# Attention and softplus FFN on one core: four buffers in place of two for the tile of reciprocals

## Chip, cores and metric

One core of a Trainium2 chip runs the whole program. The metric is the device time of one launch in microseconds (us); the median of several launches is compared. Engines are named as the profile names them: PE (TensorE matmul), PEld (TensorE weight load), DVE (VectorE), ACT (ScalarE), POOL (GpSimd), SP (SyncE, which issues nearly all DMAs).

## What is computed

Windowed attention over 8 batches, 8 heads, 576 tokens and head size 64, and behind it a feed-forward block with softplus on 4608 tokens. Float32 throughout.

```python
scores = scale * np.matmul(q, k.transpose(0, 1, 3, 2))        # heads 0-3: the last 32 keys;
scores = np.where(masks, scores, -1e9)                        # heads 4-7: every 4th of the last 128
attn = np.exp(scores - max) ; attn = attn / (attn.sum() + 1e-09)
x = (attn @ v) -> [4608, 512]
h = x @ w_in                                                  # 512 -> 2048
g = np.maximum(h, 0.0) + np.log1p(np.exp(-np.abs(h)))
out = g @ w_out                                               # 2048 -> 512
```

## The kernel before, in words

**Precision by parts.** A float32 operand of the feed-forward block is split into a high and a low part of the type fp32r, and a product takes three matmuls: high by high, high by low, low by high. Each of these matmuls has a stationary operand of 128x128 and a moving operand of 128 partitions by 512 columns (2048 bytes in a partition). In what follows "moving" is the operand that `matmul` gets as `rhs` (L228).

**Stages.** The 4608 tokens are nine chunks of 512. Chunks 0 to 2 are done plainly, in 48 slots (`RUNS`, L43: a chunk and one of 16 blocks of the hidden layer). A slot is twelve matmuls `h_ps<-xh/xl,parts` (`h_part`, L659), then ScalarE and VectorE make the softplus and its parts gh and gl (`activated` L672, `softplus` L679, `early_high` L1141, `g_low` L693), and two slots later (`LAG`) twelve matmuls `o_ps<-gh/gl,parts` (`o_matmuls`, L717). The first slots stand in an order written out by hand (`OPENING`, L93), which also decodes the weights; the rest is planned.

Chunks 3 to 8 are done as three supers of two chunks with a seven-product scheme for block matrices (`PRODUCTS`, L798). A super has 56 units of twelve matmuls (`unit`, L1258): 28 of the first half (moving operand: a block of x, `x<-a_h`, `y<-s_l` and so on) and 28 of the second half (moving operand g: `x<-g,ring`, `y<-g,ring`, `z<-g,ring`). Units are numbered on from super to super, so the second halves are units 28 to 55, 84 to 111 and 140 to 167. The weights of a unit come by DMA into one of five ring tiles. In a second half the two parts of the moving operand rotate over three pairs of tiles by u%3 (`moving_of`, L1248, with the tags of `MOVING`, L1227). Of the twelve matmuls of a unit, eight read the high part and four the low part (L1266).

```python
MOVING = (("w15_1", "n1"), ("n2", "n3"), ("n4", "n5"))      # L1227: high part, low part
for wp, xp in ((0, 0), (0, 1), (1, 0)):                      # L1266: xp is the part of the moving operand
```

Couples of attention groups of later chunks run in between as visits to TensorE (`s_ps`, `a_ps`), and jobs that prepare sums of weight blocks (`job`, L1068) run on GpSimd, VectorE and ScalarE and are stored by DMA (`w_t<-cast`).

**Order.** Everything behind the opening is a `Task` with a cost, options of engines and keys that it reads and writes; `planned` (L1459) puts them in order once, and each engine keeps that order. For the reciprocals the keys are ("ri", 0) and ("ri", 1) (L1026 and L1037): the divisor of a group is planned behind the normalisation that last read its key.

**The tile that the change touches.** `divisor` (L434) writes ri (128x8 float32, 32 bytes in a partition) with `reciprocal` (L442). It is read by `divide` (L444, in the opening, always with `nc.vector` there: the words `Pv` of `OPENING`) and by `normalized` (L548).

**Where tiles lie.** The pools are opened in the order `const`, `wk`, `dec`, `ep`, `gp` (L130 to L136) and lie one behind the other in each partition, each tag with as many places as it has buffers. At `switch` (L1231) `dec`, `ep` and `gp` are closed and `late` is opened where `dec` began. In bytes of a partition:

- `const`: begins at 1152 = 9 x 128, behind a DMA scratch of 1024 and four constants of 32. Its tags take 2816 (k2), 2560 (k), 2048 or 4096 bytes, all multiples of 128. Among them are xh and xl, the blocks of x, the ring tiles, all g_of tiles, the spare e on xl01 and w15_1.
- `wk`: nm, sm and ri, two buffers of 32 each, and mask, two buffers of 1024.
- `dec`: three buffers of 2048 for a. `ep`: two of 2048 for e of the slots. `gp`: pt, gh and gl (two each), g_x and g_y, 2048 or 2560 each.
- `late`: n0 (the other spare e), n1 to n5, 4096 each but n2 on its first use as d (2048). n1 to n4 serve the last six jobs first (b, d and cast), then n1 to n5 are g tiles.

Of the kernel before, what the change touches and what calls it, by code (L numbers as in the profile page):

```python
# [14 lines left out]
F32 = mybir.dt.float32  # L15
# [9 lines left out]
P = 128  # L25
# [8 lines left out]
NB = 2 * CH // P  # L34
# [81 lines left out]
def tile_windowed_attention_softplus_ffn(  # L116
# [15 lines left out]
    wk = ctx.enter_context(tc.tile_pool(name="wk", bufs=2))  # L132
# [23 lines left out]
    def pin(ins):  # L156

        tc.keep_in_program_order(ins)
        pinned[0] = ins
# [154 lines left out]
    class Group:  # L314
# [118 lines left out]

        def divisor(self):  # L434
            sm = self.sm
            self.ri = ri = wk.tile([P, NB], F32, name="ri")
            pin(nc.vector.tensor_scalar(
                out=sm, in0=sm, scalar1=1.0e-9, scalar2=1.0, op0=ALU.add, op1=ALU.mult
            ))
            if self.planned:  # L440
                sm, ri = sm.rearrange("p (r t h) -> p h t r", r=2, t=2), ri.rearrange("p (h t r) -> p h t r", h=2, t=2)
            pin(nc.vector.reciprocal(out=ri, in_=sm))  # L442
# [343 lines left out]
    for word in OPENING.split():  # L786
        name = word[:3] if word[0] == "D" and word[1] != "l" else word.rstrip("0123456789_")
# [856 lines left out]
```

## Time and profile before

| what | us |
|---|---|
| median of 3 runs | 829.82 |
| the runs | 828.8, 829.82, 832.06 |
| the profiled execution | 830.7 |
| its span, first to last instruction | 828.9 |
| TensorE matmul busy, of the span | 808.5 (98%) |
| VectorE busy | 663.9 (80%) |
| ScalarE busy | 500.8 (60%) |
| GpSimd busy | 188.3 (23%) |

The profile is one execution. Busy time of PE is the time in which at least one matmul was in the pipeline, and the duration of a single matmul (some 390 ns) overlaps with its neighbours'; how fast the matmuls follow one another is read from the chain of work that ended last, where consecutive matmuls of one output are merged to one piece with their count and the time that they took on the chain. Releasers of waits are inferred from semaphores. DMA share is the mean busy share of the core's 16 DMA engines.

### The profile page before, as it was taken

Reading aid. Unit: us, or ns where it says so; the run is one execution under the profiler, and the core shown is the slowest. Engines: PE = TensorE matmul, PEld = TensorE weight load, DVE = VectorE, ACT = ScalarE, POOL = GpSimd, SP = SyncE. Lnnn points to the kernel's source line nnn. Section 1 sums busy time; section 2 is a strip of 40 time slices with the busy share of each in tenths; the row PEclk is TensorE's granted clock in tenths of the full one; section 3 lists DMA queues with packets and bytes.
Section 4 is the critical chain, followed back from the end, with each engine's and each line's share of the span. In section 5 each row is a group of like instructions: output and inputs, shape, how many; then the busy total and the mean of one; then the engine's idle time right before and its main releaser. Section 6 shows DMA issues by size and latency. Waiting matters only on the chain.

```text
span 828.9 us, 19650 instructions
## 1 busy us (share of the span) xinstructions
PE 808.5 (98%) x7834; PEld 651.6 (79%) x7835; DVE 663.9 (80%) x967; ACT 500.8 (60%) x1122; POOL 188.3 (23%) x132
## 2 busy tenths in 40 slices
PE   6699999999999999999999999999999999999998
PEld 3577888888888888888777888888888888888886
DVE  5699899966687866898889887897997946768974
ACT  5587778745666644597786413888933516774410
POOL 0000000053043224655213202202024302222410
PEclk7899999999999999999999999999999999999999
DMA  9589994668879773999988999879988675655563
GB/s 330 192 290 357 368 314 132 231 209 267 276 236 290 229 214 135 361 348 368 336 292 285 327 335 323 300 234 345 304 271 291 226 243 190 202 186 196 183 214 136
DMA packets 118490, 218.94 MB, mean 264 GB/s; under 512 B 11520, under 2 KB 53632, under 8 KB 118400
## 3 DMA queue, kind: packets, MB, share of 16 engines
q1 hardware_dynamic: 117968, 216.97, 77.5%
q8 instruction: 62, 1.02, 0.5%
q10 hardware_dynamic: 432, 0.72, 0.3%
q14 instruction: 28, 0.23, 0.1%
HBM read 162.07 MB, written 55.57 MB: 263 GB/s over the span
## 4 chain that ended last, share of the span: by engine, by line
PE 89%; DMA 4%; DVE 3%; ACT 2%; issue 1%; SPq 0%; ACTq 0%; DVEq 0%
PE y L229 22%; PE o_ps L229 17%; PE h_ps L229 16%; PE z L229 14%; PE x L229 14%; PE s_ps L229 3%; PE a_ps L229 3%; DMA w_t<-cast 2%; DMA v<-vp 1%; DVE g_of L928 1%; DVE g L928 1%; DMA raw<-w 1%; DMA x_full<-rows 1%; ACT e L1296 1%; ACT s L425 1%
## 5 line engine op out<-in xcount | busy, mean ns | idle before, releaser
L928 POOL TENSOR_TENSOR g_of<-g_of 128x1024 f32<-128x1024 f32 x33 | 79.3, 2403 | 263.9 <-DVE g_of L1299 133.9
L928 DVE TENSOR_TENSOR g<-g_of,g 128x1024 fp32r<-128x1024 f32 x84 | 122.3, 1462 | 16.0 <-ACT g L960 15.2
L960 ACT CAST g<-g_of 128x1024 fp32r<-128x1024 f32 x61 | 63.7, 1047 | 111.2 <-PE z L229 42.6
L229 PE MATMUL o_ps<-gh,parts 128*128 128x512 f32 x384 | 130.8, 399 | 0.0
L229 PE MATMUL h_ps<-xh,parts 128*128 128x512 f32 x384 | 129.7, 396 | 0.0
L229 PE MATMUL y<-g,ring 128*128 128x512 f32 x432 | 102.5, 395 | 0.0
L1296 ACT ACTIVATE e<-e 128x1024 f32<-128x1024 f32 x96 | 101.1, 1057 | 1.7
L229 PEld LDWEIGHTS y<-g,ring 128*128 128x128 f32 x432 | 80.9, 188 | 19.0
L928 POOL TENSOR_TENSOR b<-parts 128x512 f32<-128x512 f32 x29 | 40.7, 1403 | 217.5 <-DVE parts L223 148.3
L229 PEld LDWEIGHTS o_ps<-gh,parts 128*128 128x128 f32 x384 | 71.9, 187 | 17.8
L229 PEld LDWEIGHTS h_ps<-xh,parts 128*128 128x128 f32 x384 | 72.7, 189 | 16.5 <-DVE e L681 0.4
L425 ACT ACTIVATE s<-s,nm 128x64 f32<-128x64 f32 x224 | 74.8, 336 | 6.7 <-DVE nm L416 6.7
L229 PE MATMUL o_ps<-gl,parts 128*128 128x512 f32 x192 | 75.8, 395 | 0.0
L229 PE MATMUL h_ps<-xl,parts 128*128 128x512 f32 x192 | 75.6, 394 | 0.0
L229 PE MATMUL x<-g,ring 128*128 128x512 f32 x288 | 68.2, 395 | 0.4 <-DVE g L928 0.4
L229 PE MATMUL z<-g,ring 128*128 128x512 f32 x288 | 68.1, 394 | 0.1
L229 PEld LDWEIGHTS x<-g,ring 128*128 128x128 f32 x288 | 53.9, 188 | 13.4 <-DVE g L928 0.8
L229 PE MATMUL z<-s_h,ring 128*128 128x512 f32 x192 | 63.2, 390 | 1.2 <-DMA ring<-w_b 1.2
L229 PEld LDWEIGHTS z<-g,ring 128*128 128x128 f32 x288 | 54.0, 188 | 13.1 <-DVE g L928 0.6
L928 DVE TENSOR_TENSOR g_of<-y,temp 128x512 f32<-128x512 f32 x60 | 39.9, 684 | 30.1 <-PE y L229 29.9
L229 PE MATMUL y<-s_h,ring 128*128 128x512 f32 x192 | 63.7, 392 | 0.0
L229 PE MATMUL x<-a_h,ring 128*128 128x512 f32 x192 | 63.3, 391 | 0.0
(111 smaller groups left out, 1517.7 us busy)
## 6 DMA issues: line engine op xcount, KB each, us to landing
ring<-w_t SPq DMA_DIRECT2D x96, 512.0 KB, 4.2
ring<-w_b SPq DMA_DIRECT2D x72, 512.0 KB, 4.7
raw<-w SPq DMA_DIRECT2D x64, 256.0 KB, 5.8
w_t<-cast SPq DMA_DIRECT2D x64, 256.0 KB, 5.1
w_b<-parts SPq DMA_DIRECT2D x48, 256.0 KB, 4.3
v<-vp SPq DMA_DIRECT2D x14, 512.0 KB, 5.3
x_full<-vp SPq DMA_DIRECT2D x14, 512.0 KB, 6.2
turned<-sq SPq DMA_DIRECT2D x112, 64.0 KB, 3.2
```

Of the source, the lines that this page charges most:

```text
L229: tc.keep_in_program_order(nc.tensor.matmul(**kw))
L425: pin(nc.scalar.activation(out=self.blocks[:, t], in_=src, func=AF.Exp, bias=self.nm[:, t : t + 1], scale=1.0 / 8.0 if self.masked else 1. ...
L928: pin((nc.gpsimd if name == "POOL" else nc.vector).tensor_tensor(out=dst, in0=a, in1=b, op=op))
L960: pin(nc.scalar.copy(out=dst, in_=src))
L1296: pin(nc.scalar.activation(out=to(), in_=of(), func=func, **kw))
```

## The change

The tile ri is given four buffers of its own in place of the pool's two. In a partition `wk` becomes 2 x 32 = 64 bytes longer, and all tiles of `mask`, `dec`, `ep`, `gp` and `late` move up by 64 bytes. Nothing else is changed.

```diff
         def divisor(self):
             sm = self.sm
-            self.ri = ri = wk.tile([P, NB], F32, name="ri")
+            self.ri = ri = wk.tile([P, NB], F32, name="ri", bufs=4)
```

## Rows read from the trace of the kernel before

**Rows 1.** The page: busy us (share) xinstructions by engine; the chain by engine.

```profile
PE 808.5 (98%) x7834; PEld 651.6 (79%) x7835; DVE 663.9 (80%) x967; ACT 500.8 (60%) x1122; POOL 188.3 (23%) x132
...
PE 89%; DMA 4%; DVE 3%; ACT 2%; issue 1%; SPq 0%; ACTq 0%; DVEq 0%
```

**Rows 2.** Waits of PE and PEld, 80 to 829 us: us, times, longest us.

```profile
PE z L229 <- DMA ring<-w_b: 1.2, 1, 1.2
...
PEld z L229 <- DVE temp L928: 1.6, 1, 1.6
PEld x L229 <- DVE g L928: 0.8, 1, 0.8
```

**Rows 3.** Busy us (instructions) PE, PEld, DVE, ACT, POOL; PE clock; DMA share; GB/s.

```profile
320.00:330.00 10.00, 10.00 (x45) 8.07 (x44) 8.23 (x10) 5.71 (x9) 7.16 (x5) 1.00 0.12 44
...
340.00:350.00 10.00, 10.00 (x106) 8.12 (x107) 9.05 (x14) 5.95 (x8) 4.70 (x5) 1.00 1.04 401
...
405.00:445.00 40.00, 38.29 (x404) 29.84 (x403) 35.24 (x46) 28.41 (x58) 9.61 (x4) 1.00 0.86 299
...
420.00:440.00 20.00, 19.87 (x85) 15.82 (x86) 19.97 (x25) 15.66 (x25) 2.41 (x1) 1.00 0.80 274
```

**Rows 4.** The chain, start us and us: matmuls on blocks of x.

```profile
333.12 2.74 PE x L229 x12
...
670.90 2.76 PE x L229 x12
673.66 2.72 PE z L229 x12
...
709.02 2.72 PE x L229 x12
```

**Rows 5.** The chain: early slots, both products.

```profile
165.70 2.80 PE o_ps L229 x12
168.50 2.74 PE h_ps L229 x12
...
200.55 2.80 PE o_ps L229 x12
```

**Rows 6.** The chain: the last second half, 28 units on g in seven rows.

```profile
747.10 11.14 PE x L229 x48
758.24 11.10 PE z L229 x48
769.34 11.15 PE y L229 x48
...
813.88 11.15 PE y L229 x48
```

**Rows 7.** The tile ri: ns min/median/max, first and last start us, forms.

```profile
L442 DVE RECIPROCAL ri<-sm x36: 202/204/206, 14.5 to 614.5; 128x8 f32<-128x8 f32 x36
L554 DVE TENSOR_TENSOR normal<-a_ps,ri x28: 637/681/693, 162.4 to 624.1; 128x512 f32<-128x512 f32 x28
L445 DVE TENSOR_TENSOR s<-s,ri x8: 681/684/693, 14.8 to 71.0; 128x512 f32<-128x512 f32 x8
```

**Rows 8.** The chain: first and last piece of 60 o_ps matmuls before 81 us.

```profile
48.44 2.80 PE o_ps L229 x12
...
78.07 2.30 PE o_ps L229 x9
```

**Rows 9.** Tiles e and g, ns min/median/max; the page's group: busy us, mean ns.

```profile
L1296 ACT ACTIVATE e<-e x96: 1039/1061/1067, 345.2 to 752.0; 128x1024 f32<-128x1024 f32 x96
...
L928 DVE TENSOR_TENSOR g<-g_of,g x84: 1170/1220/3458, 411.4 to 817.8; 128x1024 fp32r<-128x1024 f32 x84
...
L928 DVE TENSOR_TENSOR g<-g_of,g 128x1024 fp32r<-128x1024 f32 x84 | 122.3, 1462 | 16.0 <-ACT g L960 15.2
```

**Rows 10.** DMA issues: count, KB each, median us from issue to landing.

```profile
w_t<-cast SPq DMA_DIRECT2D x64, 256.0 KB, 5.1
w_b<-parts SPq DMA_DIRECT2D x48, 256.0 KB, 4.3
```

## The prediction, made before the changed kernel ran

> **What bounds the kernel now.** I read the busy times and the chain first, then TensorE's waits, then the busy times by stretch, and last the chain piece by piece. The first two say that TensorE is the bound: it is busy 98% of the span and holds 89% of the chain [rows 1]. From 80 us to the end the longest of its waits on other engines and DMAs are 1.2 us of matmuls and 1.6 us of weight loads [rows 2]. So a nanosecond taken off a big matmul after 80 us is a nanosecond off the end, unless an engine behind it cannot follow. In 405:445 one cannot: TensorE is busy 38.29 of 40 us there, and within it, in 420:440, VectorE is busy 19.97 of 20 [rows 3].
>
> The piece-by-piece chain is the view that decides this case. Every big matmul is 128x128 by 512 columns, and they come in twelves. The reader is to compare the time of twelve:
> - twelve on blocks of x (the first halves of the supers): 2.72 us [rows 4];
> - twelve of the output projection of the early slots (o_ps): 2.80 us, and the twelve h_ps after them 2.74 us [rows 5];
> - 48 in the second halves of the supers (moving operand g): 11.14, 11.10 or 11.15 us [rows 6], where four times 2.72 would be 10.88.
>
> [...] What differs is where the moving operand lies. The x blocks and xh, xl lie in `const`; gh and gl lie in `gp`; g lies in `late`, but for one of its six tiles, which is w15_1 in `const`. By the sizes of the tiles, `const` ends on a multiple of 128 bytes, `wk` takes 6 x 32 + 2 x 1024 = 2240 = 17 x 128 + 64 bytes, and so every tile of `dec`, `ep`, `gp` and `late` begins 64 bytes past a multiple of 128, and none of `const` does.
>
> The rows test this against the rival reading, that a freshly written operand is slow. Units of twelve rotate over three pairs of g tiles. With u%3 = 1 or 2 both tiles are in `late`; with u%3 = 0 the high part, read by 8 of 12 matmuls, is w15_1. If only the address counts, a full `late` unit costs 2.80 and a u%3 = 0 unit 2.72 + 0.08 x 4/12 = 2.747. The last second half starts at unit 140, so its seven groups of four hold one, two, one, one, two, one, one units of the cheap kind. That gives 3 x 2.80 + 2.747 = 11.147 or 2 x 2.80 + 2 x 2.747 = 11.094. The rows are 11.14, 11.10, 11.15 and, at the end, 11.15; the three left out there are 11.14, 11.10, 11.15 [rows 6]. Seven of seven fall as the address says, while w15_1 is written just before its use like the others. **So 64 bytes off cost 80 ns in twelve matmuls, 6.7 ns in each.**
>
> **The change part by part.**
> - *Four buffers of ri.* `wk` grows by 2 x 32 bytes to 2304 = 18 x 128. The readers of ri are the product at L445 and the normalisation at L554, both on VectorE, and so is its writer L442 [rows 7]: reuse of a buffer was already ordered by that engine, so no wait goes. The planner's keys are still ("ri", 0) and ("ri", 1), so its order stays. No instruction and no DMA is added or moved past a queue. 0 us; there is nothing to hide.
> - *Early slots.* RUNS has 48 slots, each with twelve h_ps and twelve o_ps. Sixty o_ps matmuls, five slots' worth, stand before 80 us [rows 8]; 43 slots come after. A pair costs 2.80 + 2.74 = 5.54 [rows 5] and should cost 2 x 2.72 = 5.44; the 0.02 on h_ps is the change-over from a shifted operand, seen as 2.76 too in the first twelve after a g phase [rows 4]. 43 x 0.10 = **4.3 us**. If the 0.02 belongs to h_ps itself, it is 43 x 0.08 = 3.4.
> - *Opening, five slots.* TensorE shares the chain with other engines there; between 0 and 5 x 0.10 = 0.5 I take the middle, **0.25 us**.
> - *Second halves of the supers.* The last one runs 813.88 + 11.15 - 747.10 = 77.93 us [rows 6] against 28 x 2.72 = 76.16: 1.77 us. Three of them: 5.3, and with the change-over of the x twelves behind them (2.76 and 2.74 against 2.72 [rows 4]) **5.4 us**.
> - *What VectorE takes back.* In 420:440 it is full [rows 3], so units 28 to 35 can't come sooner by their own saving: 8 x 1.77/28 = 0.5 us lost: **-0.5 us**; nothing lost if VectorE's waits shrink with TensorE's. What is late next there is the low part of g.
> - *VectorE, ScalarE, GpSimd.* e lies alternately at a shifted and at an unshifted address in the supers, yet all 96 activations take 1039 to 1067 ns [rows 9]. 0 us, with at most 28/1061 of a ScalarE that does not bind.
> - *The DMA-full stretch from 340 us* (share 1.04 [rows 3]) could swallow the 4.3 us won before it. But the DMAs are at share 0.12 in 320:330, and fill only when TensorE leaves the early slots. I count no loss; the rival below prices it.
> - *DMAs that touch the moved pools.* Of the 64 transfers w_t<-cast, 24 read a `late` tile. The nearest rows, 256 KB each, are 5.1 us to landing for these and 4.3 us for w_b<-parts, which reads `const` alone [rows 10]. So the bounds are 24 x 0.8 = 19 us of landing time either way, and it lies beside TensorE as long as a block is stored before the ring loads it back. I take 0, because the two rows differ in stage and share as much as in address. If that cover were gone, it would show in the stretch of rival 1.
>
> Sum: 4.3 + 0.25 + 5.4 - 0.5 = 9.45 us, against the profiled execution of 830.7 us (span 828.9 and 1.8 around it). That execution is 0.1% above the median of the runs, 829.82, so I take the sum from the median: **820.4 us**.
>
> [...] The trace shows 2.72 against 2.80 for the same twelve at two addresses. [...]
>
> **The rivals.**
> 1. *The win before 333 us is lost at 405:445.* If DMAs and VectorE there keep their time of day, TensorE waits for ring and g, and only the later savings count: 5.4 - 0.5 = 4.9, so **824.9 us**. For it: TensorE idles there already [rows 2, 3]. Against: the DMAs are nearly empty just before [rows 3].
> 2. *The change does nothing to the matmuls.* The address is not the cause, but something else that `gp` and `late` share, such as lying last in the partition: **829.8 us**. Against it stands w15_1; for it, that one tile is the only witness inside one phase.
> 3. *Slower: VectorE and GpSimd meet more often.* The place is the subtraction that makes the low part of g: 1220 ns at the median, 3458 at worst [rows 9], when GpSimd's sums run beside it. A meeting that nothing covers costs 2.24 us. More than 9.45/2.24, so five, uncovered new ones turn the sign; eight give 17.9 - 9.45 = 8.5 us more, **838 us**. Against it: the 84 instructions already lose (mean 1462, [rows 9]) 84 x 0.24 = 20 us, and TensorE's waits on VectorE come to a few microseconds at most [rows 2].
>
> **How the numbers follow.** About 0.5% is what a measurement of this kernel can tell from no change: 4.1 us, so faster means below 825.7. Forecast 0.82; rival 1 0.10; rival 2 0.05; rival 3 0.03. Nearly all of the first and about 0.06 of rival 1 are faster: 0.88. Rival 2 and the rest of rival 1 are the same: 0.09; slower 0.03. The low end is the sum with no loss to VectorE and the opening whole (4.3 + 0.5 + 5.4 = 10.2, 819.6) less a little for the runs' scatter: 818.8. The high end takes in rival 1 at its own figure: 825.
>
> **What would show it.** Right: o_ps and h_ps in twelves of 2.72, 48 on g in 10.88, VectorE's and ScalarE's durations as before, the last second half 1.8 us shorter, and TensorE's wait near 405:445 about 0.5 us longer. Wrong: twelves on g still at 2.80 (rival 2); a new TensorE wait of some 4 us in 405:445 (rival 1); low parts of g above 1462 ns in the mean with TensorE waiting for them (rival 3).

## The result, and the profile after

The changed kernel takes 820.52 us at the median (818.43 to 822.06), beside 829.17 us for the kernel before on the same chips: a ratio of 0.9891 with a 95% interval of 0.9871 to 0.9911. The forecast was 820.4 us. One execution further down, of the kernel with everything on a multiple of 256, took 1322.09 us at a mean granted clock of 0.556; its ratio goes by the three others, and no chain of it is shown, because the trace is of that one.

The profiled execution of the changed kernel spans 818.7 us. Its page first, busy time by engine and the chain by engine, to be read against [rows 1]:

```profile
span 818.7 us, 19651 instructions
PE 799.4 (98%) x7835; PEld 651.8 (80%) x7835; DVE 660.3 (81%) x967; ACT 501.0 (61%) x1122; POOL 189.9 (23%) x132
...
PE 89%; DMA 5%; DVE 3%; ACT 1%; issue 1%; POOL 0%; SPq 0%; POOLq 0%; DVEq 0%; ACTq 0%
```

TensorE is as much the bound as before, with 9.1 us less of busy time. The instructions are the same and stand in the same order on every engine. (The one matmul more is a record that the trace before lacks.)

The chain piece by piece, start us and us, shows where the time went. The early slots, against [rows 5], the first halves, against [rows 4], and the last second half, against [rows 6]:

```profile
165.93 2.72 PE h_ps L229 x12
168.65 2.72 PE o_ps L229 x12
...
179.53 1.41 PE a_ps L229 x91
180.94 2.97 PE o_ps L229 x12
183.91 2.72 PE h_ps L229 x12
...
328.51 2.72 PE x L229 x12
...
662.50 2.72 PE x L229 x12
...
738.66 10.88 PE x L229 x48
749.54 10.88 PE z L229 x48
...
803.94 10.89 PE y L229 x48
```

Every twelve that neither follows a visit nor waits now costs 2.72 us, whatever its moving operand: o_ps 2.80 before, four twelves on g 11.10 to 11.15 before. The change-over pieces of 2.74 and 2.76 are gone as well, but for one of 2.74 behind a visit.

TensorE's waits from 80 us on, against [rows 2], and the durations of the tiles e and g, against [rows 9]:

```profile
PE z L229 <- DVE temp L928: 0.7, 1, 0.7
PE z L229 <- DVE g L928: 0.5, 1, 0.5
...
PEld z L229 <- DVE temp L928: 1.1, 1, 1.1
```

```profile
L1296 ACT ACTIVATE e<-e x96: 1040/1060/1067, 340.8 to 743.5; 128x1024 f32<-128x1024 f32 x96
...
L928 DVE TENSOR_TENSOR g<-g_of,g x84: 1173/1218/3332, 406.7 to 807.8; 128x1024 fp32r<-128x1024 f32 x84
```

No longer wait took the place of the saving, and the other engines' instructions last as long as before. The saving is TensorE's alone.

Two pieces of the chain tell how the two executions compare in time: the first o_ps begins at 48.44 us before [rows 8] and here at

```profile
47.44 2.73 PE o_ps L229 x12
```

So 1.0 us of the 10.2 us between the two spans arose before any matmul that the forecast speaks of; it is a difference between two executions. That leaves 9.2 us, and the medians differ by 8.65 (7.4 to 10.7 by the interval of the ratio).

### The profile page after: what moved, and what is told of

It is laid out like the page before. It is cut to its first block, busy times and chain, and to the rows that moved or that the text cites. A ratio compares the mean times of both kernels' runs of the same rounds, so it can differ in the third digit from the quotient of the medians.

```text
span 818.7 us, 19651 instructions
## 1 busy us (share of the span) xinstructions
PE 799.4 (98%) x7835; PEld 651.8 (80%) x7835; DVE 660.3 (81%) x967; ACT 501.0 (61%) x1122; POOL 189.9 (23%) x132
## 4 chain that ended last, share of the span: by engine, by line
PE 89%; DMA 5%; DVE 3%; ACT 1%; issue 1%; POOL 0%; SPq 0%; POOLq 0%; DVEq 0%; ACTq 0%
PE y L229 24%; PE o_ps L229 15%; PE h_ps L229 15%; PE z L229 15%; PE x L229 15%; PE a_ps L229 3%; PE s_ps L229 3%; DMA v<-vp 1%; DMA raw<-w 1%; DMA ring<-w_t 1%; DMA ring<-w_b 1%; DVE g_of L928 1%; DMA x_full<-rows 1%; DVE g L928 1%; DVE g_of L1299 0%
## 5 line engine op out<-in xcount | busy, mean ns | idle before, releaser
L928 DVE TENSOR_TENSOR g<-g_of,g 128x1024 fp32r<-128x1024 f32 x84 | 121.5, 1453 | 14.8 <-ACT g L960 14.3
L229 PE MATMUL o_ps<-gh,parts 128*128 128x512 f32 x384 | 128.9, 394 | 0.0
L229 PE MATMUL y<-g,ring 128*128 128x512 f32 x432 | 100.4, 390 | 0.0
```

The source lines that it names most:

```text
L229: tc.keep_in_program_order(nc.tensor.matmul(**kw))
L928: pin((nc.gpsimd if name == "POOL" else nc.vector).tensor_tensor(out=dst, in0=a, in1=b, op=op))
```

## The experiments

The forecast's theory was that a moving operand off a multiple of 128 bytes costs 6.7 ns a matmul. Four kernels were made to tell it from two rivals: that the buffers do it, and that the pools `gp` and `late` are slow for another reason.

**The pad without the buffers.**

```diff
     wk = ctx.enter_context(tc.tile_pool(name="wk", bufs=2))
+    wk.tile([P, 16], F32, name="pad", bufs=1)
...
             self.ri = ri = wk.tile([P, NB], F32, name="ri")
```

> Two buffers of ri as before, and an unused 64-byte tile at the head of wk, so that dec, ep, gp and late lie as in the changed kernel. Theory (the address of the moving operand is the whole of it): twelve o_ps in 2.72 us, 48 matmuls on g in 10.88, the time of the changed kernel, 820.5 us, ratio 0.989. Rival (the two further buffers of ri free something): twelve o_ps at 2.80, 48 on g at 11.10 to 11.15, 829 us, ratio 1.00.

Measured: 819.96 us, ratio 0.9894 (0.9879 to 0.9908). The chain:

```profile
168.83 2.72 PE o_ps L230 x12
...
749.06 10.88 PE z L230 x48
```

The two further buffers of ri do nothing that shows; moving the pools by 64 bytes gives the whole change.

**The buffers, and the pools off again.**

```diff
     wk = ctx.enter_context(tc.tile_pool(name="wk", bufs=2))
+    wk.tile([P, 16], F32, name="pad", bufs=1)
...
             self.ri = ri = wk.tile([P, NB], F32, name="ri", bufs=4)
```

> Four buffers of ri, and the unused 64-byte tile on top, so that the moved pools lie 64 bytes past a multiple of 128 again (128 bytes above their place before). Theory: twelve o_ps in 2.80, 48 on g in 11.10 to 11.15, 829 us, ratio 1.00. Rival (the buffers count): 820.5 us, ratio 0.989. A third reading, that the pools only had to leave the exact place that they had: 820.5 too, with twelves at 2.72.

Measured: 826.38 us, ratio 0.9974 (0.9958 to 0.9991): slower than the changed kernel, but not all the way back. The chain:

```profile
189.36 2.76 PE o_ps L230 x12
192.12 2.77 PE h_ps L230 x12
...
674.63 2.72 PE y L230 x12
...
745.36 11.04 PE x L230 x48
```

Again 64 bytes past a multiple of 128, yet twelve o_ps cost 2.76, not 2.80, and 48 on g 11.02 to 11.04 in all seven groups. The price is not one price for "off". And the time is won on g alone: in the early slots the h_ps behind cost 2.77 instead of 2.74, so that a pair takes 5.53 us, where it took 5.54 before.

**The pad moved to `const`.**

```diff
+    const.tile([P, 16], F32, name="pad", tag="pad")
     opened = const.tile([P, 704], F32, name="opened", tag="k2")
...
             self.ri = ri = wk.tile([P, NB], F32, name="ri")
```

> Two buffers of ri, and the unused 64-byte tile at the head of const, so that const lies 64 bytes past a multiple of 128 and dec, ep, gp and late on one. Theory: the price changes sides. Twelve h_ps and twelve on blocks of x cost 2.80, o_ps 2.72 and the u%3 = 1 and 2 units on g 2.72, the u%3 = 0 units 2.72 + 0.08 x 8/12 = 2.77. Against the changed kernel's 820.5 us that is (48 + 84) x 0.08 = 10.6 us and 28 x 0.053 = 1.5 us more, 832.6 us, ratio 1.004. All weights lie in const: if the stationary operand's address counted too, o_ps and g would be dear as well, and the time would be 840 us or more. Rival (only gp and late are sensitive, say for lying last in the partition): 820.5 us.

Measured: 828.40 us, ratio 1.0004 (0.9986 to 1.0021), and the price did not change sides. The chain:

```profile
188.67 2.80 PE o_ps L230 x12
191.47 2.74 PE h_ps L230 x12
...
675.84 2.72 PE y L230 x12
...
746.56 11.14 PE x L230 x48
```

None of the times in the text came (832.6, 840 or more, 820.5). This fells the theory. The blocks of x lie 64 bytes off and still take 2.72; gh, gl and the g tiles lie on multiples of 128, as in the changed kernel, and take 2.80. The reading that `gp` and `late` are slow as such falls with the first experiment, where the same pools are fast. What orders all five layouts is the distance in a partition from the start of the weights, which lie in `const`, to that of the moving operand. Weight slices begin at multiples of 512 bytes of their tile, so the distance modulo 256 (what is left of it after whole steps of 256 bytes) is that of the tiles: 0 wherever 2.72 was seen, 192 wherever 2.80 was seen (before: 64 - 128; here: 128 - 192), and 64 for the 2.76. That became the second theory.

**Everything on a multiple of 256.**

```diff
+    const.tile([P, 32], F32, name="pad", tag="pad")
     opened = const.tile([P, 704], F32, name="opened", tag="k2")
```

> The changed kernel with an unused 128-byte tile at the head of const, so that every pool lies on a multiple of 256 bytes; in the changed kernel all of them lie 128 past one. Theory (a multiple of 128 is enough): 2.72 and 10.88 stay, 820.5 us, ratio 0.989. Rival (a coarser line than 128 bytes counts): twelve matmuls below 2.72; if 128 bytes off cost as much as 64 did, 2.64, which over some 264 twelves of the big matmuls would take 20 us off, 800 us.

Measured: 820.27 us, ratio 0.9897 (0.9881 to 0.9914). A common shift of 128 bytes changes nothing, and the 800 us of a coarser line did not come. Both theories expect that.

**Everything off by 64, together.** Made to tell the two theories apart by 21 us. The pad of 64 bytes at the head of `const`, in the changed kernel:

```diff
+    const.tile([P, 16], F32, name="pad", tag="pad")
     opened = const.tile([P, 704], F32, name="opened", tag="k2")
...
             self.ri = ri = wk.tile([P, NB], F32, name="ri", bufs=4)
```

> The changed kernel with the unused 64-byte tile at the head of const: const and all later pools lie 64 bytes past a multiple of 128 together, weights and moving operands alike. First theory (a moving operand off a multiple of 128 costs 6.7 ns a matmul): every twelve of the big matmuls costs 2.80, the time of the changed kernel plus (48 + 48 + 168) x 0.08 = 21 us, 841 us, ratio 1.015. Second theory, formed on the swap run (what counts is the distance between the moving operand and the weights that are read beside it, and 0 modulo 256 is a good one): 2.72 and 10.88 throughout, 820 us, ratio 0.989.

Measured: 820.34 us, ratio 0.9895 (0.9867 to 0.9923). The chain:

```profile
168.99 2.72 PE o_ps L230 x12
...
750.44 10.88 PE z L230 x48
```

No operand of a big matmul lies on a multiple of 128, and each is as fast as in the changed kernel. The absolute address, as far as these shifts of 64 and 128 bytes go, does not count.

**Only the weights moved.** The counterpart: all moving operands stay where the change put them, modulo 256, and the ring tiles, the weights of the supers, are 256 bytes longer and are read from 64 bytes further on.

```diff
-            ring[n] = const.tile([P, 2, 2, HALF], F32R, name="ring", tag=RING_HOMES[n])
+            ring[n] = const.tile([P, 2 * CH + 64], F32R, name="ring", tag=RING_HOMES[n])[:, 16 : 16 + 2 * CH]
+            ring[n] = ring[n].rearrange("p (a b c) -> p a b c", a=2, b=2)
```

> The changed kernel with only the weights of the supers moved: each of the five ring tiles is 256 bytes longer and is loaded and read 64 bytes from its start; every moving operand stays on its multiple of 128, and the early slots' weights (parts) stay too. First theory (address of the moving operand): nothing changes, 2.72 and 10.88, 820.4 us, ratio 0.989. Second theory (distance of moving operand and weights modulo 256): twelve on blocks of x and on g cost 2.80 as at the same distance of 192 in the kernel before, o_ps and h_ps stay at 2.72, and the time is 820.4 + 168 x 0.08 = 833.8 us, ratio 1.006, or some 1 us more where x and g now lag behind other engines less.

Measured: 831.87 us, ratio 1.0030 (1.0013 to 1.0046). The chain:

```profile
189.67 2.72 PE o_ps L229 x12
192.39 2.72 PE h_ps L229 x12
...
679.87 2.80 PE x L229 x12
...
749.87 11.20 PE x L229 x48
```

The supers' twelves cost 2.80 on x and on g alike, although no moving operand moved; the early slots, whose weights did not move, stay at 2.72. **The second theory is shown from both sides: move the moving operand alone, or the weights alone, and the price comes; move both, and it is gone.** The sum of 13.4 us came out as 11.4 above the changed kernel. The traces show about 1 of the 2 us between them: TensorE waits less for others at this pace. In 405:445 (busy us of PE, PEld, DVE, ACT, POOL, clock, DMA share and GB/s) it is busy 39.87 of 40 us, where the changed kernel has 38.84 at about the same work, in 400:440. First the changed kernel, then this one:

```profile
400.00:440.00 40.00, 38.84 (x408) 30.52 (x408) 36.34 (x47) 28.41 (x58) 10.12 (x5) 1.00 0.89 304
...
405.00:445.00 40.00, 39.87 (x411) 31.33 (x410) 37.27 (x48) 28.39 (x60) 11.67 (x5) 1.00 0.86 295
```

**Which distances are good.** Three scans and a control read gh, gl and the g tiles n2 to n5 from an offset inside longer tiles, the weights left alone; w15_1 and n1 stay at distance 0. So a unit on g is of one of three kinds by u%3: both parts at 0, or at either of two offsets. The edit of the first; the others differ in the six numbers:

```diff
+SLOT_OFF = (16, 128)
+LATE_OFF = {'n2': 32, 'n3': 32, 'n4': 96, 'n5': 96}
...
-        return gpool.tile([P, CH], F32R, name=f"g{part}", tag=f"g{part}{i % 2}")
+        at = SLOT_OFF[i % 2] // 4
+        return gpool.tile([P, CH + 64], F32R, name=f"g{part}", tag=f"g{part}{i % 2}")[:, at : at + CH]
...
+        at, n = LATE_OFF[tag] // 4, math.prod(shape[1:])
+        part = pools["late"].tile([P, 2 * CH + 64], dtype, name=name, tag=tag)[:, at : at + n]
```

> The changed kernel with gh, gl and the g tiles n2 to n5 made 256 bytes longer and read and written from an offset: slots of even number 16 bytes, of odd number 128, u%3 = 1 units 32, u%3 = 2 units 96; the weights stay. Known so far, as moving operand minus weights modulo 256: 0 costs 2.72 us for twelve, 64 costs 2.76, 192 costs 2.80. First theory (absolute address, multiple of 128): 128 costs 2.72, 16, 32 and 96 cost 2.80. Second theory (distance): 16 and 32 between 2.72 and 2.76, 96 and 128 between 2.72 and 2.84, or below 2.72 if 0 is not the best distance. If only whole multiples of 64 were told apart, 16 and 32 would cost 2.72.

The chain of the first scan, a slot at 128 and one at 16, then three groups of four units, with two of kind 0, two of 32 and two of 96 in turn:

```profile
189.12 2.79 PE o_ps L231 x12
...
194.64 2.78 PE o_ps L231 x12
...
756.83 11.10 PE z L231 x48
767.93 11.15 PE y L231 x48
779.08 11.14 PE x L231 x48
```

A group has four units, two of one kind and one of each of the others. The three groups sum to 33.39, four times the sum of one unit of each kind, 8.35; so the kinds cost 2.75 (both parts at 0), 2.80 (32) and 2.79 (96). Distance 128 is at 2.79 and not at 2.72: a multiple of 128 isn't enough. 16 and 32 (2.78 and 2.80) lie above the 2.76 that the second theory allowed them. One launch took 829.3 us.

> As the scan before with other offsets: slots of even number 4 bytes, of odd number 48, u%3 = 1 units 160, u%3 = 2 units 224. First theory (absolute address): all four cost 2.80. Second theory (distance): 4 costs 2.72 to 2.73, 48 up to 2.76, 160 and 224 between 2.72 and 2.84 and not above 2.80 by a smooth course through 192; below 2.72 if one of them is better than 0.

The second scan, a slot at 48 and one at 4, and the three groups:

```profile
188.65 2.80 PE o_ps L231 x12
...
194.20 2.84 PE o_ps L231 x12
...
777.71 11.15 PE x L231 x48
788.86 11.10 PE y L231 x48
799.96 11.16 PE z L231 x48
```

By the same sum 160 costs 2.81 and 224 costs 2.80; 4 bytes, where 2.72 to 2.73 was expected, are the dearest of all at 2.84. The smooth course that the text expected isn't there. One launch took 828.0 us.

> A control of the two scans: the same longer tiles, with the slots of odd number read from offset 0, those of even number from 192, u%3 = 1 units from 64 and u%3 = 2 units from 128. If offsets inside a tile act as the pools' offsets did: odd slots 2.72, even slots 2.80, u%3 = 1 units 2.76, and u%3 = 2 units 2.79 as the odd slots of the first scan at 128. If the longer tiles themselves cost something, odd slots are above 2.73.

The control, odd slots at 0 and even ones at 192, and three groups with two units of 128, of 0 and of 64 in turn:

```profile
188.48 2.72 PE o_ps L231 x12
...
193.92 2.80 PE o_ps L231 x12
...
778.24 11.12 PE x L231 x48
789.36 11.10 PE y L231 x48
800.46 11.09 PE z L231 x48
```

Offsets in a tile act as offsets of a pool, and the longer tiles cost nothing. The sum gives 2.79 at 128 and 2.76 at 64, as expected, but also 2.77 for the units at 0, more than at 64. So a price by the sum holds more than the distance: the first matmuls behind a unit of another kind are slow too. One launch took 828.36 us.

> A third scan for a distance better than 0: slots of even number read from offset 240, of odd number from 8, u%3 = 1 units from 208, u%3 = 2 units from 80, all else as in the other scans. First theory (absolute address of the moving operand): fallen, it would give 2.80 for all four. Second theory (distance, with 0 modulo 256 as the one good value among those tried): all four between 2.76 and 2.84, the run at 827 to 829 us. If one of them were below 2.72, that distance would make a faster kernel.

The last scan, a slot at 8 and one at 240, and three groups with two units of 0, of 208 and of 80 in turn:

```profile
191.23 2.81 PE o_ps L231 x12
...
196.78 2.80 PE o_ps L231 x12
...
791.45 11.08 PE y L231 x48
802.52 11.15 PE z L231 x48
813.67 11.11 PE y L231 x48
```

That is 2.81 at 8, 2.80 at 240, 2.82 at 208 and 2.78 at 80; one launch took 830.47 us, above the 827 to 829 expected, with the kernel before at 832.05 on that chip.

The starts of single matmuls in the traces tell the two shares better apart. From the sixth start in a twelve to the twelfth, behind most of the change-over, they follow one another at

| distance | ns from start to start |
|---|---|
| 0 | 226.7; behind units at 96 227.5, at 128 230.4 |
| 64 | 228.9 |
| 16 | 230.7 |
| 80 | 231.1 |
| 128 | 232.6 on g, 233.3 in slots |
| 8, 32, 48, 96, 160, 192, 224, 240 | 233.3 to 233.7 |
| 208 | 234.2 |
| 4 | 236.8 |

64 reads 228.9 in two kernels and 192 reads 233.3 in four. Of fifteen distances tried, 0 is the fastest, so no faster layout came out of this. Whole steps of 256 bytes didn't count: as its tiles are placed when it is built, the changed kernel has distances of 0, 256, 512 and 768 modulo 1024, all at 2.72.

## Why the prediction was right, and where it was not

**The number held, and so did the place.** TensorE was the bound, each o_ps and g twelve fell by up to 80 ns, nothing else changed, and no engine took the saving back. Rival 2 fell with the time. Rivals 1 and 3 did not come: no wait of 4 us appeared in 405:445, and the low parts of g take 1218 ns at the median, as before, and 1453 in the mean.

**That it held to 0.1 us is luck.** The saving was 8.65 us and not 9.45, and the kernel before ran at 829.17 beside it and not at 829.82. Of the sum, one term was a microsecond too large and another most of that too small (below). And by the theory as stated any multiple of 128 would have done; had the change left the pools at a distance of 128, where the first scan shows 2.79, the same forecast would have failed. The buffers happened to bring the distance to 0.

**The cause as stated was wrong.** The step that failed is "So 64 bytes off cost 80 ns in twelve matmuls". What costs is a distance other than 0 modulo 256 between the moving operand and the weights, at each of the fourteen tried. In the kernel before and in the changed one the two statements agree, because all weights lie in `const` and `const` was on multiples of 128; so the rows of the kernel before could not tell them apart, and the forecast's number needed only what they share. The swap run told them apart at once: the first theory gave it 832.6 us with dear h_ps and x, and it took 828.40 with dear o_ps and g.

**The test that seemed to confirm it could not tell.** The step "a u%3 = 0 unit 2.72 + 0.08 x 4/12 = 2.747" agreed with seven groups of seven. But its cheap tile, w15_1, lies in `const` beside the weights, so it is both on a multiple of 128 and at distance 0. Nor is the excess over 2.72 only a share of four matmuls: in the first scan such a unit has both parts at 0 and still costs 2.75, because its first six matmuls, behind a dear unit, are slow, and then the pace is 227 ns. In the kernel before the pace of that unit stays at 229 ns to its end, which speaks for a share of the low part as well.

**The terms of the sum.**
- Early slots, 4.3 us: too large. The chain's o_ps of 83.13 us begins at 81.77 after, 1.36 earlier, and the first x unit 4.61 earlier (333.12 against 328.51), so the stretch gave 3.25; in the trace of the pad in `wk`, with the same layout, it gave 2.8. The 0.10 holds for a pair without a visit. At a visit to TensorE a pair gives 0.05 to 0.09: 3.00 + 2.74 before, 2.97 + 2.72 after, at the same visit (183.73 and 180.94 us). And three pieces ran longer in this execution than in the one before, 0.58 us in all: the visits at 300.94 (1.41; after, from 296.61, 1.75) and at 159.21 (1.44 and 1.58), and fifteen h_ps at 85.93 (3.44 and 3.54).
- Opening, 0.25 us: 1.36 less the 1.00 that stood before the first o_ps is 0.36. Right.
- Second halves, 5.4 us, less 0.5 for VectorE. From 333.12 to 747.10 the lead grows from 4.61 to 8.44, from there to the end at 825.03 (814.83 after) to 10.20: 3.83 + 1.76 = 5.6, where 4.9 was forecast. The last half is 1.76 against 1.77 forecast. VectorE did not take its 0.5, and the sign "TensorE's wait near 405:445 about 0.5 us longer" failed: TensorE is idle 1.16 us there (38.84 of 40 busy, the line above) where it was idle 1.71 [rows 3]. Its wait ahead of one twelve z fell from 1.2 us, put down to a ring load before, to 0.7, put down to temp; and the eight units of the full VectorE begin 5.10 us earlier (419.20 and 414.10) and end 5.56 earlier (442.64 and 437.08), so they gave 0.46 of their 0.5. VectorE is as full as before, some 5 us sooner (19.96 of 20 us in 415:435, where it was 19.97 in 420:440 [rows 3]); this is the other end that the forecast had named.
- DMAs of the moved pools, 0: w_t<-cast takes 5.4 us to landing at the median where it took 5.1, and no wait of TensorE on a ring load is left. No run tells whether the address does that.
- The sum of what was measured is 3.25 + 0.36 + 5.6 = 9.2, where 9.45 was forecast: 1.05 too much in the early slots, 0.7 too little behind them.

**What stays open.** Why 0 is good, and why the others are not ordered by size, isn't settled. Whether the price needs the weight load at all was not shown: no run took it away. Only 0 and 192 were seen with all twelves of a long stretch at one distance. Mixed distances are not a plain mean: with the pools at 64, a unit whose high part is at 0 and low part at 64 goes at 230.8 ns, slower than at either (226.7 and 228.9). No run made the ring tiles longer without moving where they are read. Finer phases than those tried, and other shapes and types, weren't tried.

## What to carry to other kernels

Where TensorE is the bound and its matmuls (here fp32r, 128x128 by 512 columns) follow one another without a gap, compare the time of equal runs of matmuls by where their two operands lie; here the same twelve cost 2.72 to 2.84 us. Try a layout in which moving operands and weights begin at the same place modulo 256 bytes, and mind that a small tile in a pool ahead (here 3 x 2 x 32 bytes) shifts all that follows; an unused pad did the same as more buffers (819.96 us against 820.52). And when a row fits a rule about one operand, move the other operand too before believing it.

## What was not expected of the hardware

- The pace of fp32r matmuls of 128x128 by 512 columns went here with the distance between their two operands in a partition: 226.7 ns at 0 modulo 256, 228.9 at 64, 233.3 at 192, 236.8 at 4. The granted clock doesn't explain it: from 40 to 815 us it was 1.00 before the change and after it, and its mean over the span was 0.989 before, 0.990 after, 0.995 with the pools at 64 and 0.989 in the scan with 4.
- The dependence wasn't symmetric (64 against 192: four twelves on g of the same tiles take 11.02 to 11.04 us against 11.10 to 11.15) and had no second good place at 128 (233.3 ns in slots).
- Behind matmuls at another distance the next few were slow as well: h_ps at distance 0 cost 2.74 us a twelve behind o_ps at 192, 2.77 behind o_ps at 64, and 2.72 alone.
- An absolute start 64 bytes past a multiple of 128 cost nothing where both operands shared it: 820.34 against 820.52 us.
